# Windowed attention and channel mix on one core: the first unit in two halves, squares and value scalings also on ScalarE, and a new order of work

## The chip, the core and the metric

One core of a Trainium2 chip runs the whole program: TensorE (PE) for matmuls and transposes, VectorE (DVE), ScalarE (ACT), GpSimd (POOL), and SyncE (SP), which here only issues DMAs. The metric is the device time of one execution in microseconds, the median of the runs.

## What is computed

Two layers follow each other. The first is attention with a window of 128 positions and four sink positions that every query sees, for 4 batches, 8 heads, 768 positions and a head width of 64, all in fp32 in memory. The second is a channel mix over the joined heads (512 wide):

```
scores = q k^T / 8, kept where key < 4 or 0 <= query - key < 128
a  = softmax(scores);   x = a v                       # (4, 768, 512)
xp = x one position earlier (zeros at the first)
xk = mu_k x + (1 - mu_k) xp;   xr = mu_r x + (1 - mu_r) xp
k  = relu(xk w_k)                                     # 512 -> 1024
out = sigmoid(xr w_r) * ((k * k) w_v)                 # 1024 -> 512
```

## The kernel before

**Units.** The work is cut into 12 units of 256 positions (batch b, third T). Units 0, 3, 6 and 9 begin a batch. A unit goes through four functions.

- `prepare` casts k, q and v to bf16 (L645 to L661, L713), transposes k and q on PE (L677) and copies the transposes out of PSUM (L693). For late units a transposing DMA takes the place of both (L669).
- `attend` makes scores for two heads at a time (L773), takes their exponential on ACT (L860), multiplies by a 0/1 mask on DVE (L867), multiplies by the values on PE (L881; a column of ones gives the sums), takes the reciprocal of the sums (L908) and scales (L911), both on DVE. The sinks of earlier keys come in through a small product of their own (L754, L828 to L851).
- `mix` transposes x on PE (L930) or by DMA, copies it out (L943), subtracts the position before (L962) and forms xk and xr by one instruction for each of four channel blocks (L973), on DVE.
- `ffn` multiplies by w_k (L1021), takes the relu on ACT or DVE (L1034, L1038), squares on DVE (L1047), multiplies by w_r (L1054) with a tanh on ACT that stands for the sigmoid (L1062), multiplies by half of w_v (L1072), and joins both on DVE (L1083). SP stores 128 positions at a time (L1090).

**Memory.** Scores take two double banks of PSUM; everything else that PE writes takes turns in four single banks (L371). SBUF tiles come from small pools (L372 to L390), such as three raw tiles each of k, q and v, three of weights, three of outputs.

**The order of the work.** Nothing is scheduled on the chip. Each step is recorded with its engine and what it reads, writes, takes and holds (`Plan.op`, L170). Steps with a choice of engine carry it in `alts`, and the table `CHOICE` (L18) gives the choice by the step's number. The table `ORDER` (L67) lists for PE, DVE, ACT, POOL and SP in which order they run their steps; every engine runs its list in order and waits where a step is not ready. Both tables are written out in the file and come from a search made beforehand. `Plan.schedule` (L182) joins the five lists into one program order with its own table of costs and hands out buffers; into idle time of PE during the first 22 us it puts fill matmuls on zeros (L1096).

**The first unit.** Keys and queries of unit 0 are loaded as two groups of four heads, 256 positions each (L455, called at L480). Positions alternate between two rows of the tile, so that one run in memory is 512 bytes. All scores of unit 0 are made for 256 queries, and its x, xk and xr are complete only when all heads are done. The loads after these are, in SP's order: v of unit 0; k and q of unit 1; q of unit 2; both halves of w_k; v of unit 1; k of unit 2; half of v of unit 2; w_r; the other half; both halves of w_v; then k of unit 3 and on. Weights are cast in quarters or halves (L607): of the four quarters of w_k POOL casts the first, second and fourth and DVE the third.

**The end.** The last 128 positions are split by columns, 384 and 128 (`last_product`, L984), and SP issues both stores (L1010).

Of the kernel before, what the change touches and what calls it, by code (L numbers as in the profile page):

```python
# [9 lines left out]
BF16 = mybir.dt.bfloat16  # L10
# [8 lines left out]
    79: "POOL", 80: "POOL", 81: "POOL", 84: "ACT", 87: "ACT", 89: "DVE", 92: "DVE",  # L19
    94: "DVE", 95: "DVE", 97: "DVE", 98: "DVE", 131: "DVE", 134: "POOL", 137: "POOL",  # L20
    140: "ACT", 141: "DVE", 159: "PE/full", 171: "PE/tiles", 182: "POOL", 185: "POOL",
    187: "DVE", 191: "DVE", 195: "DVE", 241: "PE/tiles", 253: "PE/full", 264: "POOL",
    270: "POOL", 273: "DVE", 276: "ACT", 289: "DVE", 345: "POOL", 348: "POOL", 351:
    "DVE", 354: "POOL", 357: "ACT", 404: "PE/full", 416: "PE/tiles", 429: "POOL", 432:
    "POOL", 434: "POOL", 437: "DVE", 438: "ACT", 447: "DVE", 484: "PE/tiles", 496:
    "PE/full", 514: "POOL", 517: "ACT", 586: "POOL", 588: "POOL", 591: "POOL", 596:
    "ACT", 643: "PE/tiles", 655: "PE/full", 666: "POOL", 668: "POOL", 675: "ACT", 721:
    "PE/tiles", 733: "PE/tiles", 744: "POOL", 746: "POOL", 748: "POOL", 752: "ACT",
    753: "ACT", 819: "POOL", 821: "POOL", 823: "POOL", 828: "DVE", 847: "DVE", 872:
    "PE/tiles", 884: "PE/full", 897: "POOL", 901: "POOL", 904: "ACT", 923: "DVE", 948:  # L30
    "PE/tiles", 960: "PE/full", 979: "DVE", 1015: "DVE", 1019: "DVE",
# [14 lines left out]
BEGIN = {"SP": 800.0, "PE": 1260.0, "ACT": 800.0, "DVE": 930.0, "POOL": 930.0}  # L46
# [3 lines left out]
TOGETHER = 2  # L50

# [283 lines left out]
def kernel(  # L335
# [822 lines left out]
```

## Time and profile before

| | us |
|---|---|
| median of 3 runs | 168.67 (168.46 to 172.51) |
| profiled execution, its own time | 168.08 |
| span of its instructions | 166.4 |
| PE busy / DVE / ACT / POOL | 155.0 / 149.9 / 116.6 / 35.4 |
| HBM read and written | 24.12 MB and 6.29 MB |

The profiled execution is one of its own; 1.7 us of it lie outside the span. Busy is the time in which at least one instruction of an engine was running. Instructions of one engine overlap at their ends, matmuls by more than half, so that the sum of their lengths is above the busy time, and what one costs in a full queue is the step from its start to the next start, not its length.

### The profile page before, as it was taken

To read this page: it belongs to the slowest core of one execution; us is meant where nothing else is said; L and a number is where in the kernel's file an instruction comes from. 1 tells how busy PE (TensorE), PEld (TensorE's weight loads), DVE (VectorE), ACT (ScalarE), POOL (GpSimd) and SP (SyncE) were. 2 spreads that over 40 slices of the span, in tenths; PEclk is the share of its full clock that TensorE was granted. 3 is DMA by queue.
4 is the path that set the end of the run, shared out by engine and by line. 5 is a ranking of instruction groups with operands and counts; after the bars stand their busy time and mean duration, and the time that the engine had idled before them with its cause. 6 is when DMAs were issued, how large, how long until landed. Compare 5 with 4: busy or idle time off the path is not lost.

```text
span 166.4 us, 4712 instructions
## 1 busy us (share of the span) xinstructions
PE 155.0 (93%) x1858; PEld 102.4 (62%) x1858; DVE 149.9 (90%) x385; ACT 116.6 (70%) x190; POOL 35.4 (21%) x68
## 2 busy tenths in 40 slices
PE   7978678999999999999999999999998999999992
PEld 3545455665668586667567786485654664767541
DVE  7479999999899999999999999999979989995931
ACT  3388957996799999997978997783781647244111
POOL 2983332003606022134030060210210100000000
PEclk9999999999999999999999999999999999999998
DMA  4999999999898999999799999998995973301033
GB/s 133 253 373 389 241 260 328 387 360 325 198 290 230 229 246 248 195 226 197 173 234 138 161 206 197 219 207 109 209 174 113 246 199 126 121 9 63 0 132 120
DMA packets 74453, 34.38 MB, mean 207 GB/s; under 512 B 63800, under 2 KB 66112, under 8 KB 74432
## 3 DMA queue, kind: packets, MB, share of 16 engines
q1 hardware_dynamic: 74416, 34.09, 88.0%
q8 instruction: 14, 0.23, 0.6%
q14 instruction: 7, 0.06, 0.1%
q10 hardware_dynamic: 16, 0.00, 0.0%
HBM read 24.12 MB, written 6.29 MB: 183 GB/s over the span
## 4 chain that ended last, share of the span: by engine, by line
PE 35%; DVE 32%; DMA 16%; SPq 9%; issue 3%; POOL 2%; DVEq 0%; POOLq 0%
PE bank L1074 12%; DMA ks<-in_k_dram 11%; PE bank L1025 10%; DVE e L875 6%; DVE xr L973 5%; PE bank L1056 5%; SPq L431 5%; DVE x L911 4%; DVE xk L973 4%; DVE ob L1083 4%; DVE kk L1047 3%; DVE td L962 3%; DMA xt<-x 3%; DMA out_dram<-ob 3%; PE bank L681 2%
## 5 line engine op out<-in xcount | busy, mean ns | idle before, releaser
L1025 PE MATMUL bank<-xk,wk_sb 128*128 128x256 bf16 x384 | 50.9, 273 | 1.7 <-ACT rl L1035 1.0
L861 ACT ACTIVATE e<-sc 128x1024 bf16<-128x1024 f32 (+1 forms) x48 | 45.0, 966 | 4.9 <-PE sc L789 4.7
L1074 PE MATMUL bank<-wv_h,kk 128*128 128x512 bf16 x184 | 46.5, 379 | 1.4 <-DVE ob L1083 1.4
L1025 PEld LDWEIGHTS <-wk_sb 128*128 128x128 bf16 x384 | 35.6, 98 | 11.2 <-DVE wk_sb L615 1.3
L1035 ACT ACTIVATE rl<-bank 128x512 bf16<-128x512 f32 x44 | 25.8, 612 | 14.5 <-PE bank L1025 9.7
L875 DVE TENSOR_TENSOR e<-e,mask 128x1024 bf16<-128x1024 bf16 (+1 forms) x48 | 30.7, 654 | 0.3 <-ACT e L861 0.3
L1074 PEld LDWEIGHTS <-kk 128*128 128x128 bf16 x184 | 16.8, 97 | 16.3 <-issue 2.2
L1056 PE MATMUL bank<-wr_sb,xr 128*128 128x512 bf16 x96 | 24.5, 379 | 0.1
L973 DVE SCALAR_TENSOR_TENSOR xr<-td,mu_all,xt 128x256 bf16<-128x256 bf16 x48 | 24.4, 516 | 0.0
L1062 ACT ACTIVATE th<-bank 128x512 f32<-128x512 f32 x24 | 14.5, 609 | 10.9 <-PE bank L1056 9.6
L973 DVE SCALAR_TENSOR_TENSOR xk<-td,mu_all,xt 128x256 bf16<-128x256 bf16 x48 | 21.7, 479 | 0.1
L1047 DVE TENSOR_TENSOR kk<-rl 128x512 bf16<-128x512 bf16 x48 | 19.5, 425 | 0.3 <-ACT rl L1035 0.3
L911 DVE TENSOR_TENSOR x<-bank,rec 128x256 bf16<-128x256 f32 x48 | 19.4, 414 | 0.2
L1083 DVE SCALAR_TENSOR_TENSOR ob<-th,bank 128x512 f32<-128x512 f32 x23 | 15.7, 682 | 4.3 <-PE bank L1074 2.4
L894 PEld LDWEIGHTS <-e 128*128 128x128 bf16 x352 | 14.3, 97 | 3.6 <-DVE e L875 0.5
L894 PE MATMUL bank<-vb,e 128*128 128x65 bf16 x352 | 16.1, 193 | 0.3 <-ACT xt L944 0.3
L789 PE MATMUL sc<-qt,kt 64*64 64x128 bf16 (+4 forms) x496 | 12.8, 226 | 1.7 <-ACT e L861 0.9
L1056 PEld LDWEIGHTS <-xr 128*128 128x128 bf16 x96 | 8.9, 98 | 7.6
L789 PEld LDWEIGHTS <-kt 64*64 64x64 bf16 (+1 forms) x496 | 9.2, 106 | 5.7 <-issue 3.9
L714 POOL CAST vb<-vs 128x512 bf16<-128x512 f32 x10 | 7.0, 701 | 25.4 <-DMA vs<-in_v_dram 15.8
L962 DVE TENSOR_TENSOR td<-xt 128x512 bf16<-128x512 bf16 x24 | 11.6, 489 | 0.9 <-DMA xt<-x 0.7
L944 ACT COPY xt<-bank 128x512 bf16<-128x512 bf16 x15 | 8.8, 585 | 3.5 <-PE bank L935 3.0
(84 smaller groups left out, 151.9 us busy)
## 6 DMA issues: line engine op xcount, KB each, us to landing
vs<-in_v_dram SPq DMA_DIRECT2D x24, 256.0 KB, 5.7
out_dram<-ob SPq DMA_DIRECT2D x23, 256.0 KB, 3.0
ks<-in_k_dram SPq DMA_DIRECT2D x16, 256.0 KB, 4.4
qs<-in_q_dram SPq DMA_DIRECT2D x7, 512.0 KB, 5.9
qs<-in_q_dram SPq DMA_DIRECT2D x10, 256.0 KB, 5.1
ks<-in_k_dram SPq DMA_DIRECT2D x4, 512.0 KB, 9.4
w<-in_moe_w_k_dram SPq DMA_DIRECT2D x2, 1024.0 KB, 7.8
w<-in_moe_w_v_dram SPq DMA_DIRECT2D x2, 1024.0 KB, 11.0
```

Source lines behind the costliest of these rows:

```text
L789: nc.tensor.matmul(out=sc[keys, a, o0 + f0 - q0:o0 + f1 - q0], lhsT=lhs[rows, keys], rhs=qs[rows, f0:f1], start=u not in BIAS, stop=True, ...
L861: nc.scalar.activation(out=buf[ek][:, :, lo:], in_=buf[sck][:, :, lo:], func=AF.Exp, scale=scale)
L875: nc.vector.tensor_tensor(out=at, in0=at, in1=m, op=ALU.mult)
L894: nc.tensor.matmul(out=o[:, g, a, :], lhsT=e[:, a, e0:e0 + 128], rhs=rhs, start=(T == 0 and i == 0), stop=(i == len(blocks) - 1), skip_gro ...
L911: P.op("DVE", dve(256), lambda ok=ok, rk=rk, c=c: nc.vector.tensor_tensor(out=buf["x", u][:, :, 128 * c:128 * c + 128].rearrange("p g (a d ...
L973: nc.vector.scalar_tensor_tensor(out=buf[key][:, c, :], in0=buf[tk][:, i, :], scalar=mu[w][:, c:c + 1], in1=xt[:, c, t0 - 1:t0 + 255], op0 ...
L1025: nc.tensor.matmul(out=ps[:, i, :], lhsT=wk_sb[:, c, 128 * f:128 * f + 128], rhs=xk[:, c, :], start=(c == 0), stop=(c == NC - 1), skip_gro ...
L1035: nc.scalar.activation(out=buf[rk], in_=buf[psk].rearrange("p (i t) -> p i t", i=2), func=AF.Relu)
L1047: P.op("DVE", dve(512, 0.52), lambda f2=f2, rk=rk: nc.vector.tensor_tensor(out=buf["kk", u][:, 2 * f2:2 * f2 + 2, :], in0=buf[rk], in1=buf ...
L1056: nc.tensor.matmul(out=buf[psk], lhsT=buf["xr", u][:, c, 128 * g:128 * g + 128], rhs=wr_sb[:, c, :], start=(c == 0), stop=(c == NC - 1))
L1074: nc.tensor.matmul(out=buf[psk], rhs=wv_h[:, f, :], lhsT=buf["kk", u][:, f, 128 * g:128 * g + 128], start=(f == 0), stop=(f == NF - 1))
L1083: P.op("DVE", dve(512), lambda psk=psk, tk=tk, bk=bk: nc.vector.scalar_tensor_tensor(out=buf[bk], in0=buf[tk], scalar=1.0, in1=buf[psk], o ...
```

## The change

It has five parts.

1. **Unit 0 in halves of 128 positions.** `load_first` loads k and q for the first 128 positions of all heads, then for the second; four positions share a row, so that one run in memory is 1 KB. `attend_first`, `mix_first` and `keys_first` take the place of `attend`, `mix` and the key part of `ffn` for unit 0. Each half goes on as soon as its own x is there.
2. **Squares** (L1047) may also run on ACT, as an activation. In the new table 27 of 48 do.
3. **Value scalings** (L911) may also run on ACT, as four activations of 64 columns with the reciprocal as their scale, since ACT reads one scale per partition. 9 of 48 do.
4. **The last small store** is issued by ACT in place of SP.
5. **New tables** `CHOICE` and `ORDER` for all steps. What they assign differently: the quarters of w_k go POOL, ACT, POOL, ACT; w_r goes POOL, ACT; POOL casts v 14 times for 10, q 16 for 13 and k 11 for 13; ACT casts v 5 times for 10; 8 relus for 4 are on DVE; 8 copies of x out of PSUM for 3 are on DVE, 10 for 15 on ACT. DVE fills the constant of ones first, and POOL builds the mask of unit 0 after the other constants that used to follow it. SP's order is now: k and q of unit 0 by halves; half of v of unit 0; k and q of unit 1; the other half; q of unit 2; the first half of w_k; half of v of unit 1; the second half of w_k; the other half of v; w_r; k and v of unit 2; k of unit 3; w_v.

The diff, with the tables and repeated patterns cut:

```diff
-BEGIN = {"SP": 800.0, "PE": 1260.0, "ACT": 800.0, "DVE": 930.0, "POOL": 930.0}
+BEGIN = {"SP": 800.0, "PE": 1260.0, "ACT": 800.0, "DVE": 1050.0, "POOL": 1250.0}
...
+FIRST = 0
...
+    def quarters(t, g):
+        return t.rearrange("p h j d -> p (h j d)")[:, 512 * g:512 * g + 512].rearrange(
+            "p (h j d) -> p h j d", h=2, j=4)
...
+    def load_first(u, g, rank):
+        for name, src in (("k", k), ("q", q)):
+            key = (name, u)
+            P.op("SP", 640.0, lambda key=key, src=src: nc.sync.dma_start(
+                out=quarters(buf[key], g).rearrange("p h j d -> p h (j d)"),
+                in_=src[0, :, 128 * g:128 * g + 128, :].rearrange(
+                    "(i h) (p j) d -> p i h (j d)", j=4, h=2)), rank, service=1000.0,
...
-            load(0, "kq", -100, 0, 4)
-            load(0, "kq", -99.5, 4, 8)
+            for g in range(2):
+                load_first(FIRST, g, -100 + g / 2)
...
+    def attend_first(u, rank):
+        def scores(g, cs, sk):
+            kt, qt = buf["kt", u], buf["qt", u]
+            for c in cs:
+                for i in range(g + 1):
+                    o0 = 128 * c if g == 0 else 256 * (c % 2) + 128 * i
+                    for a in range(2):
+                        rows = slice(64 * a, 64 * a + 64)
+                        nc.tensor.matmul(out=buf[sk][:, a, o0:o0 + 128], lhsT=kt[rows, c, i, :],
+                                         rhs=qt[rows, c, g, :], start=True, stop=True)
+
+        for g in range(2):
+            for cp in range(2):
...
+                def scaled(g=g, cp=cp, ok=ok, rk=rk, view=view):
+                    for i in range(2):
+                        for a in range(2):
+                            x0 = 256 * cp + 128 * i + 64 * a
+                            nc.scalar.activation(
+                                out=buf["x", u][:, g, x0:x0 + 64], in_=view(ok)[:, i, a, 0:D],
+                                func=AF.Copy, scale=buf[rk][:, i, a, :])
...
+    def mix_first(u, rank):
+        xt, t0 = xts[0], 16
+        for g in range(2):
...
+                        for c in range(2 * cp, 2 * cp + 2):
+                            nc.vector.scalar_tensor_tensor(
+                                out=buf[key][:, c, 128 * g:128 * g + 128], in0=flat(tk)[:, c, :],
+                                scalar=mu[w][:, c:c + 1], in1=xt[:, c, s0 - 1:s0 + 127],
+                                op0=ALU.mult, op1=ALU.add)
...
+    def keys_first(u, rank):
+        for g in range(2):
+            for f4 in range(2):
...
+                        for i in range(2 * half, 2 * half + 2):
+                            f = 4 * f4 + i
+                            for c in range(NC):
+                                nc.tensor.matmul(out=ps[:, i, :],
+                                                 lhsT=wk_sb[:, c, 128 * f:128 * f + 128],
+                                                 rhs=buf["xk", u][:, c, ts], start=(c == 0),
+                                                 stop=(c == NC - 1), skip_group_check=True)
...
+            queue = nc.sync if part else nc.scalar
+            P.op("SP" if part else "ACT", 400.0, lambda bk=bk, cols=cols, n=n, queue=queue: (
+                queue.dma_start(out=out[B - 1, S - 128:S, cols], in_=buf[bk][:, 0:n])), rank,
...
+            def square(f2=f2, rk=rk):
+                nc.scalar.activation(out=buf["kk", u][:, 2 * f2:2 * f2 + 2, :], in_=buf[rk],
+                                     func=AF.Square)
...
+            P.op("DVE", dve(512, 0.52), square_dve, rank + f2, port=True,
+                 alts={"DVE": (dve(512, 0.52), square_dve, True),
+                       "ACT": (act(512) + 27.0, square, False)},
```

More of the change, by code (lines that the diff above doesn't have):

```diff
@@ L18 @@
 CHOICE = {
[L19 to L30, printed above, removed]
@@ L32 @@
+    "PE/full", 966: "ACT", 980: "DVE", 989: "ACT", 992: "DVE", 997: "ACT", 1000:
+    "DVE", 1001: "ACT", 1017: "ACT", 1020: "DVE", 1024: "DVE", 1025: "ACT",
 }
@@ L920, in mix @@
     def mix(u, rank):
+        if u == FIRST:
+            mix_first(u, rank)
+            return
         b, T = divmod(u, NT)
```

217 lines of the change are left out of this document (197 added, 20 removed), and 142 rows, old and new, of the table ORDER.

## The prediction

> **What bounds the kernel now.** I read the page first: its slices, then the chain that ended last.
>
> ```profile
> PE 155.0 (93%) x1858; PEld 102.4 (62%) x1858; DVE 149.9 (90%) x385; ACT 116.6 (70%) x190; POOL 35.4 (21%) x68
> ...
> PE   7978678999999999999999999999998999999992
> ...
> DVE  7479999999899999999999999999979989995931
> ACT  3388957996799999997978997783781647244111
> POOL 2983332003606022134030060210210100000000
> ...
> PE 35%; DVE 32%; DMA 16%; SPq 9%; issue 3%; POOL 2%; DVEq 0%; POOLq 0%
> ```
>
> No engine alone carries the span. Followed in time, the chain runs through SyncE's issues and loads to 38 us, through PE to 72, through DVE to 138, and through PE to 163; 3.3 us follow for the last stores. A busy PE here is not a full one, since matmuls overlap in the records. So I count what PE must do by intervals from the chain and the timeline: four key matmuls (L1025) step 0.44 us, four of 512 columns (L1074, L1056) 0.86, sixteen values (L894) 0.49, eight transposes 0.45, one pair of score tiles 0.46. Over the program (384, 280 with 16 shorter, 352, 176, 24 pairs, some 5 us of sinks and spreads) that is 41.9 + 62.3 + 10.8 + 9.9 + 11.0 + 5 = about 141 us. From the windows:
>
> ```profile
> 0.00:16.00 16.00, 13.02 (x123) 7.67 (x123) 11.66 (x41) 9.38 (x15) 9.29 (x28) 1.00 0.90 283
> 16.00:30.00 14.00, 10.73 (x178) 8.23 (x168) 13.42 (x32) 11.30 (x20) 4.60 (x5) 1.00 1.03 288
> 30.00:72.00 42.00, 41.68 (x533) 28.26 (x532) 40.76 (x102) 38.66 (x66) 9.90 (x16) 1.00 1.11 267
> 72.00:138.00 66.00, 64.73 (x862) 42.96 (x861) 64.14 (x164) 48.39 (x80) 11.59 (x19) 1.00 1.00 185
> 138.00:163.10 25.10, 24.87 (x176) 15.27 (x175) 19.54 (x49) 8.83 (x15) 0.00 (x0) 1.00 0.22 84
> ```
>
> Columns: length, then busy us of PE, PEld, DVE, ACT, POOL, the granted clock (full throughout), DMA share, GB/s. Up to 30 us only 43 of 384 key matmuls have run; by the steps above PE has done 12 us of work in 30. Between 30 and 138 it does about 100 to 103 in 108, so 5 to 8 us are lost, beside a DVE that is busy for 104.9 of them. From 138 on PE is full. **So the time is PE's 141 us, plus 18 lost at the start, 5 to 8 in the middle, and the tail.** The change can gain in the first two alone.
>
> The start, from the timeline:
>
> ```profile
> 16.04 2.22 POOL L615 CAST wk_sb<-w 128x1024 bf16<-128x1024 f32 x2 [2.10 <-DMA w<-in_moe_w_k_dram]
> 16.07 1.29 DVE L962 TENSOR_TENSOR td<-xt 128x512 bf16<-128x512 bf16 x1
> ...
> 18.44 0.50 PE L1025 MATMUL bank<-xk,wk_sb 128*128 128x256 bf16 x3
> ...
> 19.58 1.58 PE L1025 MATMUL bank<-xk,wk_sb 128*128 128x256 bf16 x13 [0.65 <-DVE xk L973]
> ...
> 21.45 0.68 DVE L615 CAST wk_sb<-w 128x1024 bf16<-128x1024 f32 x1
> ...
> 23.70 0.84 POOL L648 CAST kb<-ks 128x512 bf16<-128x512 f32 x1 [5.44 <-DMA ks<-in_k_dram]
> ...
> 24.49 1.03 POOL L615 CAST wk_sb<-w 128x1024 bf16<-128x1024 f32 x1
> ```
>
> The first half of the key weights lands at 16.0. Its two quarters are cast by 18.3, the third on DVE by 22.1, and the fourth only by 25.5, because it stands on POOL behind a cast that waits for keys of unit 2 until 23.7. No key matmul of the last quarter can run before that, for any unit.
>
> **The change, part by part.** Steps of DVE and ACT, start to next start, are read from merged rows (two of a kind less the length of one): square 0.34, value scaling 0.34, half-bank copy 0.34, relu or fp32 evacuation 0.60 on DVE; 0.48 for a 512-wide evacuation, 0.51 for a cast, 0.90 for a 1024-wide exponential on ACT.
>
> *Start.* The four quarters of the key weights now go POOL, ACT, POOL, ACT, and on POOL nothing that waits for a load stands between its two. The second half of the weights is issued behind 0.25 MB more (one half of v of unit 1), 0.7 us at the 390 GB/s of the busiest slice. POOL's second cast then ends near 20.5, ACT's second, behind two exponentials, a relu and two casts, near 22: 3.5 us before the 25.5 of now. The half units themselves give less: xk of unit 0 was complete near 19.5 (PE's 0.65 wait), the first half will be there before the weights land, so keys start near 17.1 instead of 18.4. Of the 3.5 us I count **3.0**. The other way stands the queue of SyncE: the output weights (wv) are now behind 0.5 MB more, since the keys of unit 3 go ahead of them, 1.3 us; the gate's weights are 0.75 MB earlier. Products start at 35.3 now; PE has keys, gates and attention of three units to do until then, so I count the 1.3 us as covered; uncovered it leaves 1.7. Bounds of the start: 0 to 4.5 gained. The early masks: POOL builds mask0 after three other constants (0.54 + 0.3 + 0.3 us), but the ones are set first and POOL starts 1.5 us sooner than its 3.24; nothing is late.
>
> *DVE.* It loses 27 of 48 squares (27 x 0.34 = 9.2) and 9 of 48 scalings (3.1), and two weight casts (1.2). It gets 4 more relus (2.4), 5 more copies of x (1.7), 2 more evacuations of k and q (1.2), one cast of v (0.3), eight mask pieces in place of four (0.5). The 8 mixing instructions of unit 0 become 16 of 128 columns, which no row shows; one costs between half of L973's step of 0.40 and all of it, I take 0.30, so 1.6 more (0 to 3.2). Net **-5.8 us**.
>
> *ACT.* 27 squares at a cast's step, 0.52 (both read SBUF): +14.0. Nine scalings become four activations of 64 columns with a scale read per partition. The nearest row is L765, 256 columns out of a bank, 388 ns long and 0.264 from start to start; four of those are 1.06, and with the columns taken off at the slope between the two exponentials (0.79 ns each) 0.45, without any overlap 1.55. I take 1.06: +9.5 (4 to 14). It loses 4 relus (2.0), 5 copies of x (2.4), 2 evacuations (1.0), one cast of k or q and five of v (3.1), and gets two weight casts (1.9). Net **+16.9** on 116.6 busy. Between 30 and 138, where ACT is busy for 87.0 of 108, some 19 squares and 8 scalings come in and 7.5 us go out: about 98.
>
> The Trainium skill, "ScalarE: Activation LUTs", section What ACT_TABLE_LOAD costs, gives 186 ns plus 0.833 per column, 93 more for a scale read by pointer, and 93 of overlap; four by that are an estimate of 0.96 us, so the sum would be by 0.9 us of ACT smaller. Its Rules for kernel authors put mul and max on VectorE, which speaks against moving squares; the rows agree on the price, 0.34 against 0.52.
>
> *POOL.* Four more casts of v, three of q, two fewer of k, the weight casts exchanged: +3.2 us on 35.4. Beside POOL's casts DVE is held up: of 96 mixing instructions (L973) 13 ran beside one and seven of these lasted 0.65 to 0.84 instead of 0.48, and the 1.29 above is a subtraction that takes 0.42 alone. By all such rows the 39 casts cost DVE some 5.4 us, 0.14 each: 0.7 for five more.
>
> *PE.* Keys of unit 0 are 64 matmuls of 128 columns at a transpose's 0.056 for 32 of 0.109, scores 24 for 16: **+0.4** (0.1 to 0.7). Fewer fill matmuls, which stood in idle time.
>
> *Middle.* With DVE at about 100 of 108 instead of 104.9 the 5 to 8 us that PE loses there should shrink; ACT at 98 takes some back, since an evacuation that comes late holds one of four banks. I count **2.3** (from 5 gained to 4 lost). What is late next is then the exchange of banks between PE and ACT.
>
> *Tail.* The smaller of the two last stores goes out from ACT's queue, so SyncE no longer issues it behind the larger (0.81 us for both): **0.3** (0 to 0.5).
>
> Sum: -3.0 - 2.3 - 0.3 + 0.4 + nothing else = -5.2. The profiled execution took 168.08 (span 166.4), so 162.9; the median of the runs is 0.6 above it, **163.5**.
>
> **Rivals.**
> 1. *The start alone, or less* (0.23). The wv weights decide when the products begin, 1.3 us later, and the middle keeps its pace because ACT's queue takes over what DVE gave up: 1.7 gained at most, 167.0 (165.5 to 168.7). For it: the page's DMA row shows 9 tenths in every slice from 4 to 37 us.
> 2. *POOL holds DVE* (0.07). If each added cast holds DVE for its whole 0.7 us, and the gate's weight cast for 1.1, DVE gets 4.6 back and the middle gains nothing: 165.8. Against it: 0.14 per cast so far. The Trainium skill, "SBUF — State Buffer", section Who interferes with whom, says that VectorE with two SBUF inputs and a GpSimd instruction that reads SBUF exclude each other for a whole instruction; by that rule it comes out this way, and the trace agrees on single casts, not on the mean.
> 3. *Slower: ACT takes DVE's place* (0.15). ACT's queue is in order, and squares and four-part scalings stand ahead of the exponentials and relus that free PSUM. With a square at its whole 0.61 and a scaling at 1.55, ACT in the middle is at 103.5 of 108, the 96% at which DVE now costs PE 5 to 8 us. Then DVE's and ACT's losses add: -3 + 7 = +4, 172.7. It decides from about 100 of 108, that is from some 1.3 us per scaling. For it: ACT is already at 9 tenths in most slices from 50 to 72 us.
> 4. *The edit does not do what it says*: the half units cannot start keys before 16 us of weights, so if the casts were no earlier, the change would be the moves between engines alone; that is the middle's term by itself, 166.4, and counted in the first rival.
>
> **How the numbers follow.** Forecast 0.55, 160.0 to 165.2. Two per cent of 168.67 is 3.4 us, about what a measurement of this kernel can tell from no change. Faster by more: the forecast and nothing of the rivals but a sliver, 0.56. Within it: rivals 1 and 2, 0.29. Slower: 0.15. Eight times in ten: 159.5 to 171.5; that leaves out most of rival 3 beyond its better half and the case where start and middle both reach their best bounds.
>
> **What would show it.** The fourth quarter of the key weights cast by 22 us, not 25.5, and key matmuls from 17; more than 60 of them before 30 us. DVE busy near 144, ACT near 133. Activations of 64 columns near 0.26 from start to start. In the middle the chain should leave DVE for longer stretches of PE. I am wrong if PE waits for ACT (relu, exponential) for several us between 30 and 138, if products start after 36.5, or if DVE stays at 97% there because POOL holds it.

## The result

The changed kernel is slower: 173.04 us (median of 8 runs, 170.32 to 175.82) beside 169.05 us for the kernel before (median of 8, 167.62 to 172.51). Runs of one program here fall into a faster and a slower group; every ratio below compares the faster runs of both, and a profiled execution that was one of the slower runs has a star in the table of the experiments. The ratio is 1.0144, 95% interval 1.0095 to 1.0194, some 2.4 us: less than the two per cent that the prediction had called the least it could tell from no change, but with an interval clear of 1. The profiled execution took 170.38 us, span 168.7, beside 168.08 and 166.4. The forecast was 163.5 us, range 159.5 to 171.5: the sign was wrong.

The page of the changed kernel, the rows that were shown of the kernel before and the row of the granted clock (the share of its full clock that TensorE was given, in tenths):

```profile
PE 154.6 (92%) x1867; PEld 104.3 (62%) x1889; DVE 146.1 (87%) x371; ACT 131.3 (78%) x238; POOL 40.1 (24%) x73
...
PE   5996757999999999999999999999999979999992
...
DVE  6258999999989999999999999999879889786731
ACT  3277996899799999999989899998994746565311
POOL 6636225102724006214123250400321010000000
PEclk9996999999999999999999999999999999999998
...
PE 51%; DMA 18%; DVE 12%; SPq 11%; ACT 2%; issue 2%; POOL 2%; DVEq 0%
```

The windows of it, in the same stretches up to 138 us (length, busy us of PE, PEld, DVE, ACT, POOL, granted clock, DMA share, GB/s):

```profile
0.00:16.00 16.00, 12.37 (x88) 7.32 (x89) 9.41 (x35) 8.37 (x14) 9.98 (x30) 0.94 0.84 262
16.00:30.00 14.00, 9.95 (x196) 8.40 (x194) 13.75 (x39) 11.97 (x20) 5.12 (x5) 0.94 1.03 295
30.00:72.00 42.00, 40.85 (x544) 28.14 (x549) 40.57 (x101) 39.95 (x70) 10.70 (x16) 1.00 0.97 255
72.00:138.00 66.00, 64.35 (x833) 43.51 (x845) 62.03 (x154) 57.49 (x109) 14.31 (x22) 1.00 1.03 196
```

The work went where the prediction had put it: between 30 and 138 us DVE is busy for 102.6 us (104.9 before; forecast about 100), ACT for 97.4 (87.0; forecast 98). PE gained nothing from it. And in the fourth slice the clock row has a 6: PE ran at half its clock for most of that slice (14.2 to 17.6 us).

To see where time went I count PE's work as the steps of the matmuls that have run, 0.42 ns per streamed column and so on, taken at the loads of their weights. It comes to 136.2 to 136.3 us in every run. I then take the **start** (until 20 us of it are done), the **middle** (the next 90) and the **tail** (the rest of the span):

| us | start | middle | tail | span |
|---|---|---|---|---|
| before | 38.7 | 97.1 | 30.6 | 166.4 |
| after | 40.0 | 98.5 | 30.2 | 168.7 |
| forecast of the change | -3.0 | -2.3 + 0.4 | -0.3 | -5.2 |
| measured change | +1.3 | +1.4 | -0.4 | +2.3 |

The split between start and middle depends on how small matmuls are weighed. Weighed by columns and by the share of the array that they use, and by nothing else (134.3 us in all), the start is longer by 2.1 us, the middle by 0.8, and the tail is shorter by 0.6. So most of the loss is in the start, and the middle has at the least gained nothing.

The start, in time (from the timelines of PE, DVE, POOL and ACT of the changed kernel, and last one line of the kernel before; start, length, engine, line, in the last bracket the idle time before and what ended it):

```profile
5.59 1.17 PE L1366 MATMUL bank<-warm 128*128 128x256 f32 x2
6.55 0.63 PE L709 MATMUL bank<-ident,kb 128*128 128x128 bf16 x4
...
8.18 0.40 PE L788 MATMUL sc<-qt,kt 64*128 64x128 bf16 x8
...
10.22 0.89 DVE L821 TENSOR_TENSOR e<-e,mask 128x256 bf16<-128x256 bf16 x4
...
15.52 0.69 DVE L728 COPY kt<-bank 128x512 bf16<-128x512 bf16 x1 [0.31 <-PE bank L709]
...
17.24 0.61 DVE L910 SCALAR_TENSOR_TENSOR xk<-td,mu_all,xt 128x128 bf16<-128x128 bf16 x2
17.76 1.39 DVE L910 SCALAR_TENSOR_TENSOR xr<-td,mu_all,xt 128x128 bf16<-128x128 bf16 x2
17.81 1.20 POOL L638 CAST wk_sb<-w 128x1024 bf16<-128x1024 f32 x1 [2.17 <-DMA w<-in_moe_w_k_dram]
19.42 0.74 PE L933 MATMUL bank<-xk,wk_sb 128*128 128x128 bf16 x8 [0.82 <-ACT xt L891]
21.14 1.91 DVE L910 SCALAR_TENSOR_TENSOR xk<-td,mu_all,xt 128x128 bf16<-128x128 bf16 x4
23.10 1.00 PE L933 MATMUL bank<-xk,wk_sb 128*128 128x128 bf16 x15 [0.83 <-DVE xk L910]
25.14 1.16 ACT L632 ACTIVATE wk_sb<-w 128x1024 bf16<-128x1024 f32 x1
```

```profile
19.06 0.47 DVE L973 SCALAR_TENSOR_TENSOR xk<-td,mu_all,xt 128x256 bf16<-128x256 bf16 x1
```

The first half of unit 0 has no head start. Its k is cast by 5.20 us, but PE is in a fill matmul until 6.55; its scores start at 8.18 (all 256 queries of the first heads: 7.22 before), its masks at 10.22 (8.93 before). Its xk is complete at 19.7 and that of the second half at 23.05; in the kernel before the whole xk of unit 0 was complete at 19.5 (the last line). While POOL casts w_k, two of DVE's mixing instructions take 1.39 us in place of 0.61, and four take 1.91 in place of 1.13. The fourth quarter of w_k, forecast for 22 us, is cast by ACT from 25.14 to 26.30. Between 17 and 30 us PE has five waits of 0.6 to 0.8 us each: three end with ACT (a copy of x, a quarter of w_k, the exponential of the sinks), two with DVE (xk, a mask). No one engine is what PE waits for.

### The profile page after: what moved, and what is told of

The parts are those of the page before. It is cut to its first block, busy times and chain, and to the rows that moved or that the text cites. A ratio compares the mean times of both kernels' runs of the same rounds, so it can differ in the third digit from the quotient of the medians.

```text
span 168.7 us, 4793 instructions
## 1 busy us (share of the span) xinstructions
PE 154.6 (92%) x1867; PEld 104.3 (62%) x1889; DVE 146.1 (87%) x371; ACT 131.3 (78%) x238; POOL 40.1 (24%) x73
## 4 chain that ended last, share of the span: by engine, by line
PE 51%; DMA 18%; DVE 12%; SPq 11%; ACT 2%; issue 2%; POOL 2%; DVEq 0%
PE bank L1337 17%; PE bank L1278 14%; PE bank L1317 8%; DMA w<-in_moe_w_r_dram 6%; DMA w<-in_moe_w_v_dram 6%; DVE e L1109 5%; PE bank L1128 4%; SPq L444 3%; DMA vs<-in_v_dram 3%; PE sc L1021 3%; DMA qs<-in_q_dram 3%; SPq L496 2%; DVE xr L1223 2%; PE bank L1185 2%; SPq L461 2%
## 5 line engine op out<-in xcount | busy, mean ns | idle before, releaser
L1278 PE MATMUL bank<-xk,wk_sb 128*128 128x256 bf16 x352 | 45.8, 273 | 0.1
L1095 ACT ACTIVATE e<-sc 128x1024 bf16<-128x1024 f32 (+1 forms) x44 | 42.3, 983 | 2.1 <-PE sc L1021 2.0
L1278 PEld LDWEIGHTS <-wk_sb 128*128 128x128 bf16 x352 | 32.9, 98 | 8.2
L1109 DVE TENSOR_TENSOR e<-e,mask 128x1024 bf16<-128x1024 bf16 (+1 forms) x44 | 29.6, 687 | 1.0 <-ACT e L1095 0.9
L1337 PEld LDWEIGHTS <-kk 128*128 128x128 bf16 x184 | 16.8, 98 | 14.6 <-issue 0.3
L1288 ACT ACTIVATE rl<-bank 128x512 bf16<-128x512 f32 x38 | 22.2, 606 | 4.6 <-PE bank L1278 4.2
L1317 PE MATMUL bank<-wr_sb,xr 128*128 128x512 bf16 x86 | 23.6, 379 | 0.8 <-DVE ob L1348 0.2
L1348 DVE SCALAR_TENSOR_TENSOR ob<-th,bank 128x512 f32<-128x512 f32 x23 | 15.6, 681 | 3.4 <-PE bank L1337 3.2
L747 POOL CAST vb<-vs 128x512 bf16<-128x512 f32 x14 | 9.7, 694 | 34.8 <-DMA vs<-in_v_dram 30.8
L1301 ACT ACTIVATE kk<-rl 128x512 bf16<-128x512 bf16 x25 | 15.4, 634 | 1.4 <-DVE rl L1292 1.3
L1146 DVE TENSOR_TENSOR x<-bank,rec 128x256 bf16<-128x256 f32 x36 | 14.4, 413 | 0.2
L1021 PE MATMUL sc<-qt,kt 64*64 64x128 bf16 (+3 forms) x480 | 12.0, 230 | 0.0
L676 POOL CAST qb<-qs 128x512 bf16<-128x512 f32 x9 | 6.4, 725 | 22.6 <-DMA qs<-in_q_dram 22.5
L1021 PEld LDWEIGHTS <-kt 64*64 64x64 bf16 x480 | 8.7, 109 | 3.5 <-issue 2.0
L680 POOL CAST qb<-qs 128x512 bf16<-128x512 f32 x6 | 4.8, 799 | 21.6 <-DMA qs<-in_q_dram 17.3
## 6 DMA issues: line engine op xcount, KB each, us to landing
w<-in_moe_w_v_dram SPq DMA_DIRECT2D x2, 1024.0 KB, 10.3
```

The lines of the kernel that those rows point to most:

```text
L1021: nc.tensor.matmul(out=sc[keys, a, o0 + f0 - q0:o0 + f1 - q0], lhsT=lhs[rows, keys], rhs=qs[rows, f0:f1], start=u not in BIAS, stop=True, ...
L1095: nc.scalar.activation(out=buf[ek][:, :, lo:], in_=buf[sck][:, :, lo:], func=AF.Exp, scale=scale)
L1109: nc.vector.tensor_tensor(out=at, in0=at, in1=m, op=ALU.mult)
L1146: nc.vector.tensor_tensor(out=buf["x", u][:, :, 128 * c:128 * c + 128].rearrange("p g (a d) -> p g a d", a=2), in0=view(ok)[:, :, :, 0:D], ...
L1278: nc.tensor.matmul(out=ps[:, i, :], lhsT=wk_sb[:, c, 128 * f:128 * f + 128], rhs=xk[:, c, :], start=(c == 0), stop=(c == NC - 1), skip_gro ...
L1288: nc.scalar.activation(out=buf[rk], in_=buf[psk].rearrange("p (i t) -> p i t", i=2), func=AF.Relu)
```

## The experiments

Theory A: the loss is that w_v comes late (its first product started at 35.3 us, now at 38.8). B: it is PE's clock. C: ACT has taken DVE's place. D: ACT's queue delays the w_k quarters. E: DVE bounds the start, and the halves give it more to do. F: the halves are neutral, the rest of the new order costs. All numbers in one table (the last two columns: the time of the profiled execution, from which start and middle are read, and when before 35 us its granted clock was at 0.5):

| | ratio to before (95%) | start | middle | profiled, us | at half clock, us |
|---|---|---|---|---|---|
| before | 1 | 38.7 | 97.1 | 168.08 | none |
| after | 1.0144 (1.0095-1.0194) | 40.0 | 98.5 | 170.38 | 14.2-17.6 |
| e1 w_v ahead | 1.0332 (1.0221-1.0442) | 43.4 | 100.1 | 175.41* | 14.2-24.5, 27.9-31.3 |
| e2 fills | 1.0232 (1.0162-1.0303) | 40.4 | 99.0 | 171.00 | 21.5-28.4 |
| e3 squares back | 1.0576 (1.0500-1.0651) | 43.5 | 104.8 | 180.25* | 14.3-24.5, 28.0-31.4 |
| e4 scalings back | 1.0412 (1.0363-1.0462) | 43.5 | 100.3 | 175.44 | 15.6-25.8, 29.2-32.7 |
| e5 more fills | 1.0164 (1.0109-1.0218) | 41.8 | 100.0 | 173.48* | none |
| e6 casts on POOL | 1.0381 (1.0314-1.0448) | 46.0 | 100.0 | 178.02* | 16.5-19.9, 30.2-33.6 |
| e7 e5 and e6 | 1.0331 (1.0282-1.0380) | 42.5 | 99.0 | 173.25 | 25.3-28.7 |
| e8 before, few fills | 1.0116 (1.0059-1.0174) | 41.9 | 98.9 | 173.23* | 11.5-18.3, 28.6-32.0 |
| e9 first unit whole | 1.0519 (1.0470-1.0567) | 46.3 | 99.4 | 177.99 | 21.2-28.0 |
| e10 halves alone | 1.0431 (1.0383-1.0478) | 46.8 | 97.8 | 177.17 | 16.1-22.9, 29.7-33.1 |
| e11 moves alone | 1.0098 (1.0061-1.0135) | 39.5 | 99.2 | 170.83 | none |
| e12 narrow masks | 1.0097 (1.0062-1.0133) | 39.3 | 98.7 | 169.80 | 24.4-27.8 |
| e13 squares only | 0.9994 (0.9966-1.0023) | 38.9 | 98.3 | 168.74 | none |
| e14 late moves | 1.0034 (0.9996-1.0071) | 38.3 | 99.0 | 169.34 | none |
| e15 split mixing | 1.0197 (1.0131-1.0263) | 43.0 | 100.0 | 175.40* | 20.1-30.4 |
| e16 short fills | 1.0101 (1.0062-1.0141) | 39.4 | 98.1 | 169.50 | 14.6-18.0, 24.8-28.2 |
| e17 late scalings back | 1.0212 (1.0130-1.0294) | 44.9 | 100.6 | 177.41* | 17.0-20.4, 23.8-34.0 |
| e18 before, short fills | 1.0074 (1.0023-1.0125) | 39.3 | 98.0 | 169.94 | 9.5-16.3 |

Start, middle and clock are of one profiled execution each. How far two executions may differ is seen in e17, which does the same as the changed kernel up to 65 us and yet has a start of 44.9 us for 40.0, with 13.7 us at half clock for 3.4.

**e1: w_v earlier.**

```diff
-        1, 0, 3, 2, 4, 6, 7, 5, 16, 8, 10, 9, 11, 12, 15, 17, 18, 19, 13, 14, 20, 24,
+        1, 0, 3, 2, 4, 6, 7, 5, 16, 8, 10, 9, 11, 12, 15, 13, 17, 18, 14, 19, 20, 24,
```

> The changed kernel, but SyncE issues the first half of the output weights w_v ahead of both halves of v of unit 2 and the second half ahead of the keys of unit 3. Theory A (the start is lost since w_v comes late and the products with it): w_v is issued near 21.5 and 26.5 us instead of 27.6 and 29.3, the first product of the output (L1337) starts near 38 instead of 43, and the time falls by 1.5 to 3 us, to 168 to 169.5 on a profiled execution, ratio to the kernel before 0.995 to 1.005. Theory B (the clock) or C (ACT has taken DVE's place): products earlier, but the time within 0.7 us of the changed kernel, 170.4, ratio 1.010 to 1.016.

The first half of w_v landed at 29.6 us in place of about 37. Its casts on DVE came no earlier (40.1 for 37.0): by then DVE's queue was late, after a start with 13.7 us at half clock. The time rose in all runs. So w_v by itself is not borne out as what holds, though the edit also sends v of unit 2 and k of unit 3 later. In the changed kernel the chain that ended last does run through SyncE's issues and then through the loads of w_r (15.5 to 26.3 us) and w_v, by this line of it:

```profile
29.33 10.35 DMA w<-in_moe_w_v_dram
```

But DVE was idle for only 0.26 us ahead of its casts of w_v there, so other work was nearly as late.

**e2, e5: fill matmuls that hold the clock.** In e5, behind the steps named:

```diff
+                unit, at, n = {130: (0, 2, 4), 133: (0, 2, 2), 150: (1, 0, 3), 220: (1, 2, 2),
+                               172: (1, 2, 3)}.get(i, (0, 0, 0))
+                for _ in range(n):
+                    self.fill(self.buf["sc", unit, at][:, 0, :], 1)
```

> The changed kernel with five more matmuls on zeros in TensorE's idle time: two of 512 fp32 columns behind the key transposes of unit 1 (11.9 us) and three of 512 bf16 columns behind its query transposes (13.7 us); they go to a score bank that is free then. Theory B (the start is lost since the granted clock falls to 0.5 between 14 and 18 us): the granted clock stays at 1.00 from 12 to 20 us, 64-wide scores of unit 1 go from 0.85 back to 0.54 us, and the time falls by 1 to 1.5 us, ratio to the kernel before 1.005 to 1.009. Theories A and C: the clock recovers but keys still wait for the cast quarters of w_k and products for w_v, so the time stays within 0.5 us of the changed kernel, ratio 1.011 to 1.017.

> The changed kernel with fourteen more matmuls on zeros (512 bf16 columns, 0.22 us each), in score banks that are free then: four behind the key transposes of unit 1 (11.9 us), two behind its query transposes, three behind the second transposes of x of unit 0 (18.6 us), two behind the keys of its second half (24 us), three behind the sinks of unit 1 (25.6 us). In the earlier run five of them, of other sizes, had kept the granted clock at 1.00 at 14 us, and it fell at 21.5 us instead, for 6.9 us. Theory B (an underfed TensorE lowers its own clock, and that is most of the loss): no stretch at 0.50 before 35 us, and the time falls by 1 to 2.5 us from the changed kernel's 170.4, ratio to the kernel before 0.998 to 1.007. If the clock is a by-product of waits that would be there anyway: the clock holds, but the time stays at 170 to 171, ratio 1.010 to 1.018.

In e2 the clock held at 14 us and fell at 21.5 for 6.8 us. In e5 it held throughout, in the profile and, to 0.996 or better, in every run, and the ratio is 1.0164, not below that of the changed kernel. So holding the clock in this way wins nothing: either the fallen clock is a small part of the loss, or the fourteen fills cost as much as they bring. The runs do not tell the two apart.

**e8: what the clock costs.** `P.fill_until` of the kernel before from 22000 to 8000.

> The kernel before, with its matmuls on zeros ended at 8 us of its plan in place of 22: it loses the four that ran from 8.8 to 9.9 us and at 15.3 us, and nothing else. They compute nothing. Theory B: the granted clock falls to 0.50 for 3.4 us or a multiple of it somewhere between 10 and 25 us, and the time rises by 1.5 to 5 us, ratio 1.009 to 1.03. Otherwise: the clock stays at 1.00, and the time within 0.4% of the kernel before.

```profile
PEclk9985898799999999999999999999999999999999
```

That is the clock row of the page of e8; in the kernel before it has nines up to the last slice. The four matmuls that went compute nothing and stood in idle time; without them the clock was at half for two stretches, and the kernel 1.2% slower (0.6 to 1.7). The clock was down in the runs behind that ratio too: their means are 0.967 to 0.988, those of the kernel before 0.988 to 1.000. The changed kernel's are 0.980 to 0.988, half as far below 1. At the price of e8 (2.0 us) its clock would cost about 1 us of the 2.4; that is an estimate.

**e6, e7: the w_k quarters earlier.**

```diff
-    79: "POOL", 80: "ACT", 81: "POOL", 82: "ACT", 83: "POOL", 84: "ACT", 85: "ACT",
+    79: "POOL", 80: "POOL", 81: "POOL", 82: "POOL", 83: "POOL", 84: "ACT", 85: "ACT",
...
-        ... 129, 132, 138, 102, 192, 79, 81, 83,
+        ... 129, 132, 138, 102, 192, 79, 80, 81, 82, 83,
```

> The changed kernel with the second and the fourth quarter of w_k cast on GpSimd, each right behind the quarter before it, and not on ScalarE. In the changed kernel ScalarE cast them at 20.1 to 21.2 and 25.1 to 26.3 us, in order behind exponentials, a relu and two casts of v. Theory D (ScalarE's queue delays the key weights): quarters ready near 20.2 and 24.0 us, exponentials and evacuations of the start about 1 us earlier each, TensorE 1 to 2 us further by 30 us, time 168.5 to 169.8, ratio to the kernel before 1.000 to 1.008. Theory B: the start gets a little denser but the clock still falls once, ratio 1.008 to 1.02.

> Both edits together: the fourteen fills and all four quarters of w_k on GpSimd. If B and D are both right and add up: 166.5 to 168.5, ratio to the kernel before 0.987 to 1.000. If D alone is right: as the run with the casts alone, ratio 1.000 to 1.008. If B alone is right: as the run with the fills alone.

The timelines of POOL, DVE and PE in e6:

```profile
17.80 2.22 POOL L638 CAST wk_sb<-w 128x1024 bf16<-128x1024 f32 x2 [1.93 <-DMA w<-in_moe_w_k_dram]
21.71 2.22 POOL L638 CAST wk_sb<-w 128x1024 bf16<-128x1024 f32 x2 [1.69 <-DMA w<-in_moe_w_k_dram]
...
17.40 0.69 DVE L728 COPY kt<-bank 128x512 bf16<-128x512 bf16 x1 [0.32 <-PE bank L709]
...
22.95 1.52 DVE L1109 TENSOR_TENSOR e<-e,mask 128x1024 bf16<-128x1024 bf16 x1
24.39 1.13 DVE L910 SCALAR_TENSOR_TENSOR xk<-td,mu_all,xt 128x128 bf16<-128x128 bf16 x4
...
25.32 1.26 PE L933 MATMUL bank<-xk,wk_sb 128*128 128x128 bf16 x16 [1.58 <-DVE xk L910]
```

The quarters are ready at 20.0 and 23.9 us, 1.2 and 2.4 us earlier than on ACT, as expected. PE then waits for DVE's xk, which is complete at 25.5 and not at 23.05, and has done 7.5 us of work by 30 us for 10.3. Most of that is not the edit: this execution was late ahead of it. DVE's copy of kt starts at 17.40 us for 15.52 in the changed kernel, so 1.9 of the 2.5 us were lost before POOL's first cast at 17.80. Beside the casts the mask then takes 1.52 us (0.68 alone). What the edit shows is the time: 1.0381 for 1.0144. D is not borne out, and with it falls the step of the prediction that the whole start hung on: earlier quarters, cast in this way, did not make the start shorter. With the fills added (e7) it is no better, 1.0331.

**e12, e16: the first half earlier.** In e12, which leaves most of the scores of unit 0 unmasked:

```diff
+                        at = at[:, :, 0:16]
-                        nc.vector.tensor_tensor(out=at, in0=at, in1=m, op=ALU.mult)
+                        nc.vector.tensor_tensor(out=at, in0=at, in1=m[:, :, 0:16], op=ALU.mult)
```

> The changed kernel, in which the eight mask multiplications of unit 0 on VectorE work on 16 columns of each block in place of 128 or 256, so that unit 0's scores stay unmasked elsewhere and its result is another. That takes about 2 us from VectorE between 10 and 14.5 us and nothing from any other engine. Theory E (VectorE bounds the start): xk of unit 0 and all that follows is 1.5 to 2 us earlier, time 168.3 to 169.3 for the changed kernel's 170.4, ratio to the kernel before 0.999 to 1.006. Rivals (the loads, the casts of the weights or ScalarE's queue bound the start): less than 0.6 us, ratio 1.010 to 1.018.

and in e16:

```diff
-                    wide = next((k for k in (4, 2) if t - now > k * one + 75.0), 1)
+                    wide = next((k for k in (4, 2) if t - now > k * one + 75.0 and now < 4000.0), 1)
...
+                    if now > 4000.0:
+                        break
```

> The changed kernel, where each of the four stretches of idle time of TensorE between 5.5 and 10 us is given one matmul on zeros of 512 bf16 columns (0.22 us) in place of fp32 ones that took 0.5 to 1.3 us and ended after the step behind them was ready: the key transposes of the first half at 6.55 us, whose cast ended at 5.20, the first scores at 8.18, the query transposes of the second half at 9.04, the first values at 10.83. If the fills ate the head start of the halves: first scores near 7.2, first masks near 9, and either the time falls by 0.5 to 1.5 us (ratio 1.004 to 1.011) with the clock kept, or the clock falls earlier and for longer and takes that back (ratio 1.012 to 1.025). If they are harmless: first masks still after 10 us, ratio 1.010 to 1.018.

Both bring xk forward. In e16 the scores start at 7.25 us and the masks at 9.19; in both xk of unit 0 is complete at 20.8 us for 23.05. Both are at 1.010 for 1.0144, with intervals that overlap; PE has done 11.3 us of work by 30 us in both, for 10.3. So the traces bear E out in direction, and the times stay outside E's forecast for e12 (0.999 to 1.006) and are not told apart from the changed kernel's. Where the rest went, the timeline of PE in e12 shows (in e16 the last wait is 2.08 us):

```profile
18.92 0.62 PE L934 MATMUL bank<-xk,wk_sb 128*128 128x128 bf16 x8 [1.52 <-POOL wk_sb L638]
...
20.27 1.57 PE L934 MATMUL bank<-xk,wk_sb 128*128 128x128 bf16 x24 [0.27 <-ACT wk_sb L632]
23.87 0.40 PE L1067 MATMUL bank<-vsink,es 128*128 128x130 bf16 x4 [2.02 <-ACT es L998]
```

With xk there, PE waits first for POOL's first quarter of w_k, whose load landed at 17.7 us, and then for ACT, whose queue has run without a break from 18 us on through exponentials, w_k quarters, copies and casts. The start of the changed kernel is a place where the loads, DVE and ACT stand close behind each other, and the halves had shortened none of them.

**e15: what the halves give to DVE, in the kernel before.**

```diff
-                        nc.vector.scalar_tensor_tensor(
-                            out=buf[key][:, c, :], in0=buf[tk][:, i, :],
...
+                        n = 128 if u == 0 else 256
+                        for a in range(0, 256, n):
+                            nc.vector.scalar_tensor_tensor(
+                                out=buf[key][:, c, a:a + n], in0=buf[tk][:, i, a:a + n],
```

> The kernel before, where the eight mixing instructions of unit 0 with 256 columns become sixteen with 128 and nothing else changes. That is what the halves add to VectorE's work: by the steps of the two kernels 16 x 0.263 in place of 8 x 0.40 us, 1.0 us more between 14.9 and 23 us. Theory E (VectorE bounds the start): 0.5 to 1.2 us slower, ratio 1.003 to 1.007. If the loads or the casts of the weights bound it: within 0.2%.

```profile
15.59 0.60 DVE L975 SCALAR_TENSOR_TENSOR xk<-td,mu_all,xt 128x128 bf16<-128x128 bf16 x2
...
16.64 1.38 DVE L975 SCALAR_TENSOR_TENSOR xk<-td,mu_all,xt 128x128 bf16<-128x128 bf16 x2
...
20.84 0.60 DVE L975 SCALAR_TENSOR_TENSOR xk<-td,mu_all,xt 128x128 bf16<-128x128 bf16 x2
...
23.97 1.52 DVE L615 CAST wk_sb<-w 128x1024 bf16<-128x1024 f32 x1
```

That is DVE's timeline in e15. Eight more instructions, by their steps 1.0 us, and the kernel before loses 2.0% (1.3 to 2.6), about as much as by the whole change. In this execution the first of them starts at 15.59 us for 14.88 in the kernel before, so 0.7 us were lost ahead of the edit. Then one pair lasts 1.38 us beside POOL's cast; xk is complete at 21.4 us for 19.5; DVE's quarter of w_k follows at 23.97 for 21.45 and itself takes 1.52 us for 0.68 beside another; and PE runs at half clock for 10 us (the runs behind the ratio have mean clocks of 0.98 to 0.99, this one 0.97). I had expected 0.3 to 0.7%: the price of an instruction at the start is not its own length. How the 2.0% divide between DVE's work, POOL's casts and the clock is not shown.

**e9, e10: one part alone, by two mixed orders.** e9 is the changed kernel with `FIRST = -1` and unit 0's steps of the kernel before; e10 the kernel before with `FIRST = 0` and unit 0's steps of the changed one.

> Part 1 of the change undone alone: unit 0 is loaded, attended, mixed and multiplied as in the kernel before, and its steps stand on each engine among their neighbours by the time that the plan of the kernel before gives them. Everything else, the tables of all other steps, squares, scalings and casts, is that of the changed kernel. Theory E (VectorE is full from 10 us on, and the halves give it more work and a later x, so the halves themselves cost the start): faster than the changed kernel by 1 to 3 us, ratio to the kernel before 0.996 to 1.008. Theory F (the new order and casts of the start cost it, the halves are neutral): within 0.5% of the changed kernel, ratio 1.010 to 1.02.

> Part 1 of the change alone: the kernel before, with unit 0 in halves, whose steps stand among their neighbours by the time that the plan of the changed kernel gives them; all other steps keep the engine and order that they have in the kernel before (the last small store goes out from ScalarE). Theory E: the steps of unit 0 that VectorE does are later, ratio to the kernel before 1.006 to 1.025. Theory F: ratio 0.990 to 1.004. What I had forecast of the halves alone (keys from 17.1 for 18.4 us): ratio 0.990 to 0.995.

Both starts are 6 to 8 us longer than either kernel's. In e10 PE waits 2.4 us for a cast of v and 2.1 for a mask that now stand behind unit 0's steps; in e9 ACT casts the second quarter of w_k at 23.6 us (20.1 in the changed kernel). They can't tell E from F. They show that steps of one plan between the steps of another cost more than the whole change. The middle of e10 is 97.8 us, near the 97.1 of before, although its start is 8 us longer.

**e3, e4, e17: squares and scalings back on VectorE.** Each by a table of moves after `ORDER`, such as

```diff
+MOVED = {
+    427: ("DVE", 372), 495: ("DVE", 507), 586: ("DVE", 601), 732: ("DVE", 741), 814: ("DVE",
+    807), 890: ("DVE", 894), 954: ("DVE", 912), 966: ("DVE", 1000),
+}
```

> The changed kernel with all 27 squares of ACT back on VectorE, each at the place in VectorE's order where the plan has it. ACT loses 27 x 0.52 = 14 us, DVE gets 27 x 0.34 = 9.2 us, about 109 us of work in the 108 from 30 to 138 us. Theory C (ACT's queue has taken DVE's place): faster than the changed kernel by 1 to 4 us, ratio to the kernel before 0.99 to 1.008. Theories A and B (the moves themselves pay, the loss is at the start): DVE is over-full and the time rises by 2 to 5 us, ratio 1.025 to 1.045.

> The changed kernel with the nine value scalings of ACT back on VectorE, each at the place in VectorE's order where the plan has it. ACT loses 9 x 0.79 = 7.1 us in four instructions each, DVE gets 9 x 0.34 = 3.1 us. Theory C: a scaling on ACT stands between the sums of a head pair and the transposes that free a bank, so faster than the changed kernel by 0.5 to 2 us, ratio to the kernel before 1.002 to 1.011. Theories A and B: DVE's 3.1 us count in the middle, slower by 0.5 to 2 us, ratio 1.017 to 1.027.

> The changed kernel with the 8 scalings of units 4 to 11 back on VectorE and the one of unit 0 left on ScalarE, so that nothing differs before 60 us. In the earlier run with all nine, TensorE's clock had been at half for 11 us of the start, and its 174 to 176 us say nothing about the middle. If a scaling in four instructions costs in this order too, as it did in the kernel before (1.0% with 8 scalings beside the squares, 0.0% with the squares alone): faster than the changed kernel, ratio to the kernel before 1.002 to 1.010. If this order was made for them and VectorE is the fuller engine: ratio 1.018 to 1.03.

e3 is 5.8% slower than the kernel before, with the longest middle of all, 104.8 us: in the new order the squares cannot go back. e4 lost most of its time at the start, at half clock for 13.7 us, and the profiled execution of e17, which was made to avoid that, met the same, so that it says little of the middle. e17's 1.0212 has an interval that overlaps the changed kernel's. So nothing bears out that the scalings cost in the new order; whether they pay there is not shown.

**e11, e13, e14: squares and scalings on ScalarE in the kernel before.** The same kind of table the other way, for 25 squares and 8 scalings, for the squares alone, and for the 16 squares and 5 scalings that the plan has after 95 us.

> Parts 2 and 3 alone: the kernel before, with the 25 squares and 8 scalings of units 1 to 11 on ScalarE that the changed kernel has there, put into ScalarE's order by the times of the plan of the kernel before; nothing else moved. DVE -11.2 us, ACT +19.3 us. Forecast (the middle gains from a freer VectorE): ratio 0.980 to 0.992. Theory C (in an order that was not made for it, ScalarE takes VectorE's place): ratio 1.005 to 1.04.

> The kernel before with the 25 squares of units 1 to 11 on ScalarE, as in the run with the moves alone, but the 8 scalings left on VectorE. DVE -8.5 us, ACT +13 us. With both moves the loss was 1.0% (0.6 to 1.35). If a scaling in four instructions is what hurts (it stands between the sums of a head pair and the next transposes): ratio 0.997 to 1.004. If the squares hurt (they stand in ScalarE's queue ahead of exponentials and relus): ratio 1.006 to 1.014.

> The kernel before with only those moves to ScalarE that its plan has after 95 us: 16 squares and 5 scalings. From 72 to 138 us VectorE is busy for 64.1 of 66 us there and ScalarE for 48.4, from 30 to 72 us ScalarE for 38.7 of 42. If a move costs where ScalarE is full and pays where it is not: time 0.3 to 1.5 us below the kernel before, ratio 0.991 to 0.998, which would beat both kernels. If every move to ScalarE delays exponentials: ratio 1.002 to 1.01.

The row of the chain by engine, of e11 and of e13 (before: PE 35%, DVE 32%, DMA 16%, ACT not among them):

```profile
PE 61%; ACT 19%; DVE 11%; issue 3%; DMA 3%; SPq 1%; DVEq 0%
```

```profile
PE 67%; ACT 16%; DMA 4%; SPq 4%; DVE 4%; issue 3%; DVEq 0%
```

The squares take 7.0 us of busy time off DVE and DVE off the chain, and the time stays where it was, 0.9994 (0.9966 to 1.0023). ACT stands on the chain in DVE's place. In the changed kernel itself it does not: ACT has 2% of the chain there, and between 30 and 138 us its profile lists no wait of PE for ACT. The 8 scalings on top, four instructions each, cost 1.0%. The late moves are within the noise and beat nothing.

**e18: short fills in the kernel before**, the edit of e16.

> The kernel before with its matmuls on zeros cut as in the changed kernel's run with short fills: after 4 us one of 512 bf16 columns for each stretch of idle time. Its second scores started at 9.93 us behind 1.5 us of fp32 fills though keys and queries were there at 9.05. If the fills ate time there too and the clock holds: xk of unit 0 is complete 0.5 to 0.9 us earlier, ratio 0.992 to 0.998, a version that beats both kernels. If the clock falls, as it did when its last fills were left out (ratio 1.012): ratio 1.005 to 1.02.

The clock fell at 9.5 us, and the kernel is 0.7% slower. No version here is faster than the kernel before.

## Why the prediction was wrong

- **The start (-3.0; measured +1.3).** The failed step: "POOL's second cast then ends near 20.5, ACT's second ... near 22: 3.5 us before the 25.5 of now". POOL's second ended at 22.90, ACT's at 26.30, since ACT's queue was full, and so the fourth quarter came 0.8 us later instead of 3.5 earlier. The loads were later too: the first half of w_k landed at 17.76 us for 16.0 with the same loads ahead of it, only in another order (16.9 to 17.8 in the profiles with the new order of loads; 16.0 to 17.0, once 18.1, with the old one); the reason is not shown. And the step was the wrong one: in e6 the quarters were early and the kernel slower. In its place the runs show a start in which PE waits by turns for DVE and ACT, 0.6 to 0.8 us each: of the five waits one was for a quarter of w_k, and with xk earlier (e12, e16) others of up to 2 us take their place.
- **The halves ("xk ... the first half will be there before the weights land, so keys start near 17.1").** They started at 19.42. The first half lost about 1 us to fill matmuls on PE (e16), then stood in DVE's queue behind the second half's copy of q (9.54 to 10.2 us, itself 1.5 us late from PE), and its mixing was more work for DVE. I had priced that work rightly (0.30 us each; measured step 0.263) but put it in a sum over the whole run, where 1.6 us looked small. In e15 some 1.0 us of such work in the start went with 3.3 us (2.0%) in the kernel before.
- **The fill matmuls ("stood in idle time", costed at nothing).** The changed kernel has 12, the kernel before 17. e8 is this step by itself, in the kernel before: 1.2% for four of them. Which cover they gave, the granted clock, I had read as "full throughout" and not asked why. The Trainium skill, "TensorE: Matmul & The Clock Gate", section What's actually happening, says that the clock is halved after an idle window of 3.4 us, counted in windows that run freely. The trace agrees on the half, on the 3.4 us (stretches of 3.41, 6.83 and 10.24 us) and on windows that do not start with the program, not on the idle window: there was none (last section). By that rule the clock of the changed kernel would not have fallen: PE's longest gap ahead of the fall was 1.05 us.
- **POOL (rival 2, 0.07).** By all pairs that overlap, POOL held DVE for 7.4 us in place of 5.7, 0.9 of the 1.6 us more in the first 30 us. Forecast was 0.7 in all. The mean per cast stayed small; the longest holds in the start, 0.8 us each, are beside casts of w_k.
- **The middle (-2.3; measured between +0.8 and +1.4 by the way of counting).** The failed step: "With DVE at about 100 of 108 instead of 104.9 the 5 to 8 us that PE loses there should shrink". e13 gives DVE that room in the kernel before and changes nothing: ACT comes onto the chain. The scalings were dear as rival 3 said, but not for their length: 0.197 us per step and 0.79 per scaling, less than the 1.06 I took. What made the changed kernel's middle longer is open. One profile can differ from the next by about as much: e18, which differs from the kernel before in the first 25 us alone, has 98.0 for 97.1.
- **Right:** squares at 0.520 us a step (0.52); busy times (DVE 146.1 for 144, ACT 131.3 for 133); the tail (-0.4 for -0.3); PE's own work (+0.1, bounds 0.1 to 0.7). Of its signs of being right, 64 key matmuls did run before 30 us, more than the 60 named, but at 128 columns each they are less work than the 43 of 256 columns of the kernel before. Of its signs of being wrong, products started at 38.8 us, after 36.5.
- **Rival 3** had the sign. That its 172.7 us lie near the median of 173.04 is luck: in the runs that the ratio compares the loss is 2.4 us, not 4, and its mechanism is there in e11 and e13 alone, as an even exchange for the squares, not as a loss of 7 us. The larger part of the loss came in at the start, for which no rival of mine stood. What share of it is the halves and what the rest of the new order is left open: e15 shows that the halves' form costs by itself in the kernel before, e9 and e10 could not separate the two.

## What to carry to other kernels

Where several engines are full and PE is not, as at a start, ask what else is late if a cast comes earlier; here the next waits, of 1.5 and 2 us in e12, were for a load and for ACT. Price an added instruction by the stage it stands in, not by its share of the run, and count the two engines that hold each other (POOL's casts beside DVE) in that stage. Matmuls that compute nothing are part of the schedule: leaving four out cost the kernel before 1.2%, shortening them 0.7%, and ahead of a step that became ready early they held it by about 1 us. And ask of a trace how late it was ahead of the edit (e6, e15). Last, an order found as a whole can't be judged by parts put into another order.

## What the runs showed of the hardware

- PE's granted clock went to 0.50 before 35 us in the profiles of the changed kernel and of 14 of the 18 others, between 9.5 and 34.0 us, for 3.41, 6.83 or 10.24 us, whole multiples of 3.41. All 20 profiles show it again 2.0 to 5.2 us behind the last matmul. Within one profile all falls and rises lie on one grid of 3.41 us: in the changed kernel the falls at 14.19 and 167.78 us are 45 steps apart. The grid does not start with the program (the first falls of e4, e6 and e17 are at 15.59, 16.52 and 16.95 us).
- It didn't take 3.4 us of idle time: in the step of the grid ahead of the 23 falls before 35 us PE was busy for 0.3 to 2.2 us, and its longest gap was 0.6 to 2.4 us. Steps at the full clock that no fall followed had 1.6 us or more. The two ranges overlap, so that busy time in the records does not decide it alone.
- The same work falls for longer or shorter from run to run: e17 and the changed kernel are the same until 65 us, with 13.7 and 3.4 us at half clock.
- A wide POOL cast (1.0 to 1.2 us long) can stretch what DVE has beside it by 0.8 us: a mask from 0.68 to 1.52 (e6), a w_k cast from 0.68 to 1.52 (e15), a pair of mixings from 0.61 to 1.39 (the changed kernel). Over all pairs that overlap the mean is far less: 7.4 us over some 97 of DVE's instructions.
